# Flips, value products, narrowing and maxima's products one tile later, and scores tied behind groups, in a fused attention and two-MoE kernel

## The chip, the cores and the metric

One core of one Trainium2 chip runs the whole program. The metric is the device time of one execution in microseconds (us). Its engines are PE (TensorE, with PEld for its weight loads), DVE (VectorE), ACT (ScalarE), POOL (GpSimd) and SP (SyncE, which here issues DMAs). Each runs its own list of instructions in order and waits for the others by semaphores.

## The reference

The input is q, k, v of shape (4, 8, 576, 64) in float32 and the weights of two MoE layers in float64. What is computed:

```
q, k   = rotary(q), rotary(k)                      # cos/sin of position, per head
a      = softmax(q k^T / 8) v                      # 4 batches, 8 heads, 576 x 576
x      = a as 2304 tokens x 512
h      = max(x w1, x w2, x w3)                     # 512 -> 768, three products
y      = h w_out                                   # 768 -> 512        (first MoE)
t      = y w_in                                    # 512 -> 2048
out    = (t * sigmoid(t)) w_out                    # 2048 -> 512       (second MoE)
```

## The kernel before

**Tiles.** The attention works in 80 tiles, 20 for each batch (tiles 0 to 19 are batch 0, 20 to 39 batch 1, and so on). A tile is a batch, a pair of heads and a piece t of 128 query positions (t = 4 is half a piece: one instruction covers both heads). Batches come one after the other, each in two parts r: pieces 0 and 1 of all four head pairs, then pieces 2, 3 and 4.

**One tile.** `attention()` is a generator that gives out one tile's work at a step. `tile_scores` (lines L389 to L405) writes the scores of a tile into a PSUM tile `s`; there is only one, so the next score waits until the exponentials have read it. `tile_max` takes the row maxima on DVE (L414) and the exponentials on ACT (L421). One step later `tile_norm` takes the reciprocal (L431) and scales on ACT (L433), and `tile_move` sends the scaled exponentials by four DMAs on SP's queue into a transposed arrangement `pt` (for batches 1 to 3, which `moved(b)` says). Two steps later `tile_flip` transposes 32 x 32 blocks of `pt` on DVE (L494), and `tile_last` does the rest with PE (L483, L439). Batch 0 is transposed on PE alone (`tile_turn`, L504 to L521). When the pieces of a part are done, `av` multiplies by v (L535, L539) at the step that `av_at` gives, and writes the first MoE's input `x`.

**What is put between the tiles.** Behind each step the main loop gives out groups of the first MoE, a group being the products (L626) into one PSUM bank; a budget RATE of 8000 columns a tile sets how many, and `x_ready` from which step on a batch's part may be used. `up` evacuates its groups on ACT (L642) and DVE (L644), `down` on ACT (L668). The loop also steps through the narrowing of the second MoE's float64 weights to float32 (`narrow_w2`): load, a first step `narrow_a` on ACT (L214) and POOL (L216), a second step `narrow_b` on DVE (L225, L226), then the measuring of maxima and a store. After it `prep_w8` casts them in halves (L895 on ACT, L899 on DVE). The splits of the first MoE's output weights W_out1 into a high half (POOL, L160) and a low half (DVE, L163) are given out by `prep_wo1`. q and k are rotated on POOL (`rope_steps`, L330 ff.) and transposed (`qk_turn`, L351 to L374).

**Maxima.** `all_max` finds one maximum over 128 partitions: PE transposes the column of row maxima (L117), DVE reduces it (L119), and PE multiplies the result by a column of ones (L120) to spread it again; `scale_of` (L130 to L133) makes a scale of it.

**Order.** A scheduler decides the order of instructions on each engine from the order in which the code gives them out and a model of the engines. `tc.issue_after(x)` adds that an instruction stands behind x on its engine; `last[...]` holds the latest instruction of a kind. Pools of buffers (`Ring`) set how far ahead a step can be.

Of the kernel before, what the change touches and what calls it, by code (L numbers as in the profile page):

```python
# [17 lines left out]
P = 128  # L18
# [4 lines left out]
def fused_kernel(  # L23
# [65 lines left out]
    z64_p = right("z64_p", 3)  # L89
# [9 lines left out]
    cos_sb = once.tile([P, 9, D], F32, name="cos_sb")  # L99
    sin_sb = once.tile([P, 9, D], F32, name="sin_sb")  # L100
# [13 lines left out]
    def all_max(m):  # L114

        ps = (ps_am[0] if ps_am else ps_m).tile([P, 512], F32, tag="m", name="m")
# [4 lines left out]
        return ps[:, 256:257]  # L121

# [45 lines left out]
    class Weights:  # L168
# [68 lines left out]
        def scale(self, nm, lo=0, n=None, ma=None):  # L237
# [3 lines left out]
            self.s, self.inv = scale_of(all_max(m1), 1, nm, const)  # L241
            return self.s, self.inv

# [59 lines left out]
    def v_scale(b):  # L303
        ma = vmax_t.pop(b)
        m = small.tile([P, 1], F32, tag="vm1", name="vm1")
        nc.vector.tensor_reduce(out=m, in_=ma, op=ALU.max, axis=AX.X)
        sv_t[b] = scale_of(all_max(m), 1, "v")

    def qk_rope(b, hp):
        t = raw_t[b, hp]  # L310
        w = w_p.tile([P, 18, D], F32, tag="w", name="w")
        if b:
            with tc.issue_after(last["pool"]):
                return rope_steps(t, w, nc.gpsimd, ((0, 6), (6, 12), (12, 18)))
# [6 lines left out]
        return rope_steps(t, w, nc.gpsimd, ((0, 6), (6, 12), (12, 18)))  # L321

    def rope_steps(t, w, eng, parts):

        tt = eng.tensor_tensor
        for lo, hi in parts:
            r, v = t[:, lo:hi, :], w[:, lo:hi, :]
            t4, w4 = (x.rearrange("p (a h) d -> p a h d", h=2) for x in (r, v))
            sin2, cos2 = (x[:, lo // 2:hi // 2, :].unsqueeze(2).to_broadcast([P, (hi - lo) // 2, 2, D]) for x in (sin_sb, cos_sb))
# [247 lines left out]
    for b in range(1, B):  # L577
        u = first[b, 0]
        for hp in range(NP):
            at(u - 10 + hp if hp < 2 else u - 4, load_v, b, hp)  # L580
            at(u - 6 + hp + hp // 2 * 2, v_max, b, hp)
        at(u, v_scale, b)

    def attention():

        back = lambda j, n: tiles[j - n] if n <= j < len(tiles) + n else None
        for j in range(len(tiles) + 4):
            if j < len(tiles):
                tile_scores(tiles[j])
                tile_max(tiles[j])  # L590
            key = back(j, 2)
# [26 lines left out]
    def group(passes, n, ps=None, more=False):  # L618
# [6 lines left out]
        for i, (l, r) in enumerate(passes):  # L625
            nc.tensor.matmul(ps[:, 0:n], l, r, start=(first and i == 0), stop=(not more and i == len(passes) - 1))  # L626
# [145 lines left out]
    def narrow_w2(W, src, nm):  # L772
# [5 lines left out]
        for n in range(M + 4):  # L778
            if n >= 4:
                W.measure(n - 4)  # L780
                if nm == "wi":
                    i, o = divmod(n - 4, 2)
# [3 lines left out]
                        in_=W.t[n - 4].rearrange("p (f n) -> p f n", n=P),  # L786
                    )
                else:
                    nc.sync.dma_start(out=zscr[nm][:, (n - 4) * 256:(n - 3) * 256], in_=W.t[n - 4])
# [23 lines left out]
        W.scale("s" + nm, n=M)  # L813
# [424 lines left out]
    copy_tables()  # L1238
# [11 lines left out]
    at(3, v_scale, 0)  # L1250
# [136 lines left out]
```

## Time and profile before

| | before |
|---|---|
| time, median of 3 runs | 998.67 us (997.64 to 1002.69) |
| the profiled execution | 997.75 us, span 996.0 us |
| PE busy | 912.6 us (92% of the span) |
| PEld busy | 671.5 us (67%) |
| DVE busy | 698.1 us (70%) |
| ACT busy | 604.4 us (61%) |
| POOL busy | 494.0 us (50%) |
| DMA moved | 146.29 MB, 147 GB/s on average |

The span is the time from the first to the last instruction in the trace; the execution is somewhat longer. An engine's busy time counts the instructions that compute, not its waits. The shares are averages over the attention with the first MoE in between (the last tile's score starts at 573.14 us) and the second MoE after it, which have different limits.

### The profile page before, as it was taken

Reading aid. Unit: us, or ns where it says so; the run is one execution under the profiler, and the core shown is the slowest. Engines: PE = TensorE matmul, PEld = TensorE weight load, DVE = VectorE, ACT = ScalarE, POOL = GpSimd, SP = SyncE. Lnnn points to the kernel's source line nnn. Section 1 sums busy time; section 2 is a strip of 40 time slices with the busy share of each in tenths; the row PEclk is TensorE's granted clock in tenths of the full one; section 3 lists DMA queues with packets and bytes.
Section 4 is the critical chain, followed back from the end, with each engine's and each line's share of the span. In section 5 each row is a group of like instructions: output and inputs, shape, how many; then the busy total and the mean of one; then the engine's idle time right before and its main releaser. Section 6 shows DMA issues by size and latency. Waiting matters only on the chain.

```text
span 996.0 us, 19123 instructions
## 1 busy us (share of the span) xinstructions
PE 912.6 (92%) x6802; PEld 671.5 (67%) x6802; DVE 698.1 (70%) x1231; ACT 604.4 (61%) x1381; POOL 494.0 (50%) x548
## 2 busy tenths in 40 slices
PE   4677998899998999988998899999998999999997
PEld 2344665566664555655655567788887888888886
DVE  5669778677677666878777646754777767756554
ACT  2878677667676766778877734463464554554442
POOL 5835495891276401623234105653678258265264
PEclk9688899999999999999999999999999999999999
DMA  6943034878896967998999855263454254334101
GB/s 149 274 145 106 13 97 113 181 145 161 194 194 160 188 121 143 210 220 185 242 212 221 186 133 192 64 222 124 154 164 133 84 166 119 110 112 133 60 1 43
DMA packets 185198, 146.29 MB, mean 147 GB/s; under 512 B 51216, under 2 KB 168720, under 8 KB 185104
## 3 DMA queue, kind: packets, MB, share of 16 engines
q1 hardware_dynamic: 183600, 144.36, 57.8%
q8 instruction: 54, 0.88, 0.4%
q10 hardware_dynamic: 1504, 0.72, 0.3%
q14 instruction: 40, 0.33, 0.1%
HBM read 90.51 MB, written 26.21 MB: 117 GB/s over the span
## 4 chain that ended last, share of the span: by engine, by line
PE 37%; DMA 7%; DVE 4%; ACT 2%; POOL 2%; issue 2%; SPq 1%; DVEq 0%; ACTq 0%; POOLq 0%
PE m L1050 8%; PE mb L1050 6%; PE c L1113 4%; PE a L1113 4%; PE b L1113 4%; PE mg L626 3%; PE m L626 3%; PE d L1113 2%; DMA w8scr<-z 2%; POOL gsum L997 1%; DMA w8s<-w8scr 1%; DMA pt<-e 1%; PE m L1018 1%; PE mb L1018 1%; PE m L1113 1%
## 5 line engine op out<-in xcount | busy, mean ns | idle before, releaser
L626 PE MATMUL m<-x,w 128*128 128x256 f16 (+1 forms) x1388 | 193.7, 289 | 11.1 <-ACT t L642 4.3
L626 PEld LDWEIGHTS <-w 128*128 128x128 f16 x1632 | 160.7, 99 | 62.9 <-issue 19.0
L1113 PEld LDWEIGHTS <-g 128*128 128x128 f16 x1485 | 145.9, 98 | 17.3
L1050 PEld LDWEIGHTS <-w8s 128*128 128x128 f16 x1344 | 131.2, 98 | 16.1 <-issue 0.9
L891 POOL TENSOR_TENSOR z<-z 128x128 f32<-128x128 f32 (+1 forms) x96 | 61.7, 660 | 134.5 <-DMA z<-zwi 56.8
L421 ACT ACTIVATE e<-s,nb 128x576 f32<-128x576 f32 x144 | 105.2, 736 | 36.7 <-DVE nb L414 35.8
L414 DVE TENSOR_REDUCE nb<-s 128x2 f32<-128x1152 f32 (+1 forms) x80 | 98.5, 1232 | 29.3 <-PE s L404 24.1
L433 ACT ACTIVATE e<-e,rec 128x576 f32<-128x576 f32 x144 | 104.2, 767 | 10.0 <-DVE rec L431 9.9
L216 POOL TENSOR_SCALAR z<-z 128x256 uint16<-128x256 uint16 x64 | 54.1, 845 | 105.9 <-ACT z L214 77.8
L404 PE MATMUL s<-T 64*128 64x512 f32 x256 | 81.1, 695 | 0.0
L494 DVE STREAM_TRANSPOSE pt<-pt 128x1024 f32<-128x1024 f32 (+1 forms) x60 | 67.8, 1130 | 16.2 <-DMA pt<-e 15.6
L539 PE MATMUL xp<-pt,vd 128*64 128x256 f32 (+1 forms) x512 | 76.5, 415 | 0.5 <-DVE pt L494 0.5
L1064 POOL TENSOR_TENSOR z<-t 128x256 f32<-128x256 f32 x32 | 27.1, 847 | 89.2 <-DVE t L1056 54.1
L1002 DVE SCALAR_TENSOR_TENSOR g<-gsum,sg,g 128x1024 f16<-128x1024 f32 x36 | 49.5, 1382 | 23.1 <-ACT g L1001 22.6
L330 POOL TENSOR_TENSOR w<-qk,sin_sb 128x384 f32<-128x384 f32 (+1 forms) x44 | 46.0, 1065 | 35.4 <-DMA qk<-in_q_dram 24.0
L1001 ACT ACTIVATE g<-gsum,sg 128x1024 f16<-128x1024 f32 x36 | 40.8, 1140 | 35.9 <-POOL gsum L997 35.9
L626 PE MATMUL m<-h,wo 128*128 128x256 f16 (+1 forms) x448 | 60.8, 286 | 0.1
L539 PEld LDWEIGHTS xp<-pt,vd 128*64 128x64 f32 x512 | 35.3, 138 | 36.5 <-issue 13.3
L626 PEld LDWEIGHTS <-wo 128*128 128x128 f16 x512 | 49.7, 98 | 15.0 <-issue 1.7
L644 DVE SCALAR_TENSOR_TENSOR t<-m,t 128x256 f32<-128x256 f32 (+1 forms) x82 | 36.7, 447 | 18.9 <-PE m L626 11.6
L1113 PE MATMUL b<-w,g 128*128 128x256 f16 x376 | 48.5, 273 | 0.0
L1113 PE MATMUL c<-w,g 128*128 128x256 f16 x376 | 48.2, 275 | 0.0
(248 smaller groups left out, 1957.5 us busy)
## 6 DMA issues: line engine op xcount, KB each, us to landing
w8s<-w8scr SPq DMA_DIRECT2D x64, 448.0 KB, 4.2
pt<-e SPq DMA_DIRECT2D x192, 128.0 KB, 3.9
z<-in_moe_w_in_dram SPq DMA_DIRECT2D x32, 256.0 KB, 3.5
z<-in_moe_w_out_dram SPq DMA_DIRECT2D x32, 256.0 KB, 3.5
w<-in_moe_w_dram SPq DMA_DIRECT2D x6, 768.0 KB, 6.2
wo<-in_moe_w_dram SPq DMA_DIRECT2D x6, 768.0 KB, 4.7
qk<-in_q_dram SPq DMA_DIRECT2D x32, 128.0 KB, 3.4
vd<-in_v_dram SPq DMA_DIRECT2D x16, 256.0 KB, 3.4
```

The lines of the kernel that those rows point to most:

```text
L216: nc.gpsimd.tensor_scalar(out=q[:, :, 2], in0=q[:, :, 1], scalar1=step, scalar2=off, op0=ALU.mult, op1=ALU.add)
L404: last["s"] = last["score"] = nc.tensor.matmul(s[:, o:o + 512], qs[r], kt[r], start=True, stop=True).ins
L414: x = nc.vector.tensor_reduce(out=nb[:, 0:m], in_=both(s, 0, 960, 576) if m > 1 else s[:, 0:576], op=ALU.max, axis=AX.X, negate=True)
L421: x = nc.scalar.activation(out=e[:, HK[g]], in_=s[:, SK[g]], func=AF.Exp, bias=nb[:, g:g + 1], accum_out=sm[:, g:g + 1])
L433: nc.scalar.activation(out=e[:, HK[g]], in_=e[:, HK[g]], func=AF.Copy, scale=r[:, g:g + 1])
L494: nc.vector.transpose(out=x, in_=x)
L539: nc.tensor.matmul(xp[r, 0:n], v4[:, g, c, :], turned(c, g), start=False, stop=(c == 3))
L626: nc.tensor.matmul(ps[:, 0:n], l, r, start=(first and i == 0), stop=(not more and i == len(passes) - 1))
L891: nc.gpsimd.tensor_tensor(out=z[:, o], in0=z[:, x], in1=z[:, y], op=op)
L1002: nc.vector.scalar_tensor_tensor(out=l, in0=x, scalar=sg_t[jb], in1=h, op0=ALU.mult, op1=ALU.subtract)
L1050: nc.tensor.matmul(o, l, r, start=(i == 0), stop=(i == len(passes) - 1))
L1113: x = nc.tensor.matmul(ps, l, r, start=first, stop=last_, skip_group_check=True)
```

## The change

Seven things are edited.

1. The flips of batches 1 to 3 come three steps after the scores instead of two (`back(j, 3)`), and the value products `av` and the first use of the MoE's input one step later for these batches. The loop has one step more.
2. A score of batches 1 to 3 stands behind the last group given out (`issue_after(last["group"])`).
3. In `narrow_w2` the first step comes two steps after the load instead of one, the second three instead of two, the measuring and store five instead of four; the float64 tiles get a fourth buffer.
4. `all_max` is cut in two. For v and for the second MoE's weights the product that spreads the maximum is given out one step later, behind the last score.
5. The tables of cosines and sines hold 5 pieces instead of 9, and the copies that filled the rest on POOL are gone.
6. A rotary step on POOL works on pieces of 8, 8 and 2 instead of three of 6.
7. For batches 2 and 3 two of the four loads of v come one step later.

```diff
-    z64_p = right("z64_p", 3)
+    z64_p = right("z64_p", 4)
...
-    cos_sb = once.tile([P, 9, D], F32, name="cos_sb")
-    sin_sb = once.tile([P, 9, D], F32, name="sin_sb")
+    cos_sb = once.tile([P, 5, D], F32, name="cos_sb")
+    sin_sb = once.tile([P, 5, D], F32, name="sin_sb")
...
+    def max_bank():
+        return (ps_am[0] if ps_am else ps_m).tile([P, 512], F32, tag="m", name="m")
+
+    def all_max_a(m, ps=None):
+
+        ps = ps or max_bank()
         nc.tensor.transpose(ps[0:1, 0:P], m, ident)
         t = small.tile([1, 1], F32, tag="amax", name="amax")
         nc.vector.tensor_reduce(out=t, in_=ps[0:1, 0:P], op=ALU.max, axis=AX.X)
+        return t
+
+    def all_max_b(t, ps=None):
+
+        ps = ps or max_bank()
         nc.tensor.matmul(ps[:, 256:257], ones, t, start=True, stop=True)
         return ps[:, 256:257]
...
-            queue.dma_start(out=t[:, 4:9, :], in_=r[:, 4:9, :])
-
-    def copy_tables():
-        for t in (sin_sb, cos_sb):
-            nc.gpsimd.tensor_copy(out=flat(t[:, 0:4, :]), in_=flat(t[:, 4:8, :]))
+            queue.dma_start(out=t, in_=r[:, 4:9, :])
...
-        sv_t[b] = scale_of(all_max(m), 1, "v")
+        vmax_t[b] = all_max_a(m)
+
+    def v_scale_b(b):
+        with tc.issue_after(last["score"]):
+            sv_t[b] = scale_of(all_max_b(vmax_t.pop(b)), 1, "v")
...
-                return rope_steps(t, w, nc.gpsimd, ((0, 6), (6, 12), (12, 18)))
+                return rope_steps(t, w, nc.gpsimd, ((0, 8), (8, 16), (16, 18)))
...
-        av_at.setdefault(len(tiles) + 2, []).append((b, hp, r))
-        x_ready[b, r] = len(tiles) + 4
+        av_at.setdefault(len(tiles) + 2 + moved(b), []).append((b, hp, r))
+        x_ready[b, r] = len(tiles) + 4 + moved(b)
...
-            at(u - 10 + hp if hp < 2 else u - 4, load_v, b, hp)
+            at(u - 10 + hp if hp < 2 else u - 4 + (b > 1), load_v, b, hp)
...
         at(u, v_scale, b)
+        at(u + 1, v_scale_b, b)
...
-        for j in range(len(tiles) + 4):
+        for j in range(len(tiles) + 5):
             if j < len(tiles):
-                tile_scores(tiles[j])
+                with tc.issue_after(last["group"]) if tiles[j][0] else nullcontext():
+                    tile_scores(tiles[j])
                 tile_max(tiles[j])
-            key = back(j, 2)
+            key = back(j, 3)
             if key and moved(key[0]):
                 tile_flip(key)
...
-        for n in range(M + 4):
-            if n >= 4:
-                W.measure(n - 4)
+        for n in range(M + 5):
+            if n >= 5:
+                W.measure(n - 5)
...
+            if 3 <= n <= M + 2:
+                with tc.issue_after(last["max"]):
+                    W.narrow_b(n - 3, part.pop(n - 3, None))
             if 2 <= n <= M + 1:
-                with tc.issue_after(last["max"]):
-                    W.narrow_b(n - 2, part.pop(n - 2, None))
-            if 1 <= n <= M:
                 if wide:
-                    W.t[n - 1] = z_p.tile([P, 256], F32, tag="z", name="z")
+                    W.t[n - 2] = z_p.tile([P, 256], F32, tag="z", name="z")
                 with tc.issue_after(exps[-1]):
-                    W.narrow_a(n - 1, part.get(n - 1), pool=True)
+                    W.narrow_a(n - 2, part.get(n - 2), pool=True)
...
-        W.scale("s" + nm, n=M)
+        t = W.scale_a(n=M)
+        yield
+        with tc.issue_after(last["score"]):
+            W.scale_b("s" + nm, t)
         yield
```

What the scheduler makes of it shows at three places. The first is PE's order at the turn from batch 0 to batch 1. Here `s_1659` is the score of tile 20 and `s_1758` that of tile 21, `tr` are transposes, `m_1601` is the maximum of W_out1 and `m_1700` that of v. Before:

```order
L401 MATMUL s_1659<-kd_0_122,T_1380 128x2x64
L404 MATMUL s_1659<-T_1380 128x512 x2
L351 MATMUL tr_1573<-ident_78,qk_855 128x128 x4
L351 MATMUL tr_1567<-ident_78,qk_855 128x128 x4
L117 MATMUL m_1601<-ident_78,wm_2_1599 1x128
L515 MATMUL tr_1673<-ident_78,e_1454 128x128 x3
L365 MATMUL tr_1579<-ident_78,qk_855 128x128
L120 MATMUL m_1601<-amax_1603,ones_79 128x1
L117 MATMUL m_1700<-ident_78,vm_1_1698 1x128
L401 MATMUL s_1758<-kd_0_122,T_1380 128x2x64
```

After, the score of tile 20 is `s_1658`; `m_1600` is the maximum of W_out1, `m_1636` and `m_1727` are two `down` groups of batch 0, `h` their input, `wo1f` and `wo` the split pieces of W_out1:

```order
L128 MATMUL m_1600<-amax_1602,ones_79 128x1
...
L650 MATMUL m_1636<-h_0_973,wo1f_140 128x256
...
L650 MATMUL m_1727<-h_5_1521,wo_0_141 128x256
L650 LDWEIGHTS wo_0_141
L650 MATMUL m_1636<-h_5_1521,wo_0_141 128x256
L423 MATMUL s_1658<-kd_0_122,T_1379 128x2x64
L426 MATMUL s_1658<-T_1379 128x512 x2
L650 LDWEIGHTS wo_0_141
L650 MATMUL m_1727<-h_5_1521,wo_0_141 128x256
```

The score of tile 20 stood ahead of the product of W_out1's maximum; now it stands behind it and behind 35 of the 36 products of two groups that read W_out1's pieces.

The second place is DVE's order near tile 58. `nb` are row maxima, `pt_4596` is the buffer of tiles 54 to 56 of batch 2 (a flip of 1024 columns, or of 512 for tile 56, the half piece), `z` are pieces in narrowing. Before:

```order
L414 TENSOR_REDUCE nb_4886<-s_4882 128x2
L494 STREAM_TRANSPOSE pt_4596<-pt_4596 128x512
L150 TENSOR_REDUCE vmax_4538<-vd_0_128 128x1
L225 TENSOR_SCALAR z_4835<-z_4835 128x256
L899 SCALAR_TENSOR_TENSOR z_1_4634<-z_1_4634,wihalf_4125 128x512
```

After, `nb_4806` is the row maximum of tile 58, `nb_4886` that of tile 59, and `pt_4536` the buffer of tiles 54 to 56:

```order
L436 TENSOR_REDUCE nb_4806<-s_4802 128x2
L516 STREAM_TRANSPOSE pt_4536<-pt_4536 128x1024
L163 TENSOR_REDUCE vmax_4458<-vd_0_128 128x1
L238 TENSOR_SCALAR z_4743<-z_4743 128x256
...
L436 TENSOR_REDUCE nb_4886<-s_4883 128x1
L516 STREAM_TRANSPOSE pt_4536<-pt_4536 128x512
```

Behind the maximum of tile 58 stood the flip of tile 56; now it is the flip of tile 55, and that of tile 56 stands behind the next maximum.

The third place is PE's order at the last maximum, that of the second MoE's W_out (`wm_0`). `m_6677` before and `mg_6880`, `mg_6915` after are groups of the first MoE, `s_6627` is the score of tile 79. Before, the lines left out are the rest of one group:

```order
L117 MATMUL m_6665<-ident_78,wm_0_6663 1x128
L626 LDWEIGHTS w1f_137
L626 MATMUL m_6677<-x_5505,w1f_137 128x256
...
L120 MATMUL m_6665<-amax_6667,ones_79 128x1
L394 MATMUL s_6627<-T_5330,qd_0_121 128x512
```

After, the lines left out are the rest of `mg_6880` and further groups up to `mg_6915`:

```order
L650 MATMUL mg_6880<-x_5504,w_0_138 128x256
L120 MATMUL m_6700<-ident_78,wm_0_6698 1x128
...
L650 MATMUL mg_6915<-x_5504,w_0_138 128x256
L561 MATMUL xp_6747<-pt_6554,vd_0_129 64x320
L128 MATMUL m_6720<-amax_6702,ones_79 128x1
```

The transpose and the product of this maximum now lie further apart, and both come after the last score.

## Rows read from the trace of the kernel before

**Rows 1.** Windows: stretch, length, busy time of each engine, PE clock, DMA share, GB/s.

```profile
core 0: us, PE busy (x) PEld busy (x) DVE busy (x) ACT busy (x) POOL busy (x), PEclk, DMA share, GB/s
152.60:572.80 420.20, 385.31 (x2537) 243.34 (x2537) 310.47 (x575) 300.18 (x832) 178.72 (x221) 0.99 0.84 182
301.90:332.50 30.60, 24.26 (x138) 13.55 (x139) 20.15 (x43) 20.03 (x59) 15.08 (x19) 0.94 0.83 178
411.20:471.70 60.50, 49.99 (x342) 33.15 (x342) 49.63 (x96) 44.70 (x124) 24.44 (x37) 0.97 0.90 206
```

**Rows 2.** PE's waits, 152.6 to 573 us: us in total, times, longest.

```profile
PE s L401 <- ACT e L421: 8.8, 7, 1.6
PE s L394 <- ACT e L421: 6.8, 5, 3.8
PE m L626 <- DVE t L644: 4.4, 4, 1.6
PE m L120 <- DVE amax L119: 3.3, 1, 3.3
...
PE m L626 <- ACT t L642: 1.8, 2, 1.2
```

**Rows 3.** DVE's waits in the same stretch.

```profile
DVE pt L494 <- DMA pt<-e: 13.8, 11, 3.0
DVE z L226 <- POOL z L216: 11.6, 8, 4.4
```

**Rows 4.** Timeline of DVE: start, duration, instruction [idle before <- releaser].

```profile
524.95 1.25 DVE L494 STREAM_TRANSPOSE pt<-pt 128x1024 f32<-128x1024 f32 x1 [1.53 <-DMA pt<-e]
...
529.90 1.35 DVE L414 TENSOR_REDUCE nb<-s 128x2 f32<-128x1152 f32 x1
```

**Rows 5.** Timeline of ACT.

```profile
434.23 0.72 ACT L895 ACTIVATE w8o<-z,wihalf 128x512 f16<-128x512 f32 x1 [2.75 <-DMA w8scr<-w8o]
...
527.63 0.44 ACT L214 ACTIVATE z<-z 128x256 f32<-128x256 f32 x1 [2.30 <-DMA z<-in_moe_w_out_dram]
```

**Rows 6.** Timeline of PE at eight places.

```profile
158.47 0.39 PE L401 MATMUL s<-kd,T 128*128 128x128 f32 x2
...
307.73 0.49 PE L401 MATMUL s<-kd,T 128*128 128x128 f32 x2 [1.59 <-ACT e L421]
...
322.45 0.38 PE L401 MATMUL s<-kd,T 128*128 128x128 f32 x1 [1.45 <-ACT e L421]
...
436.55 1.84 PE L394 MATMUL s<-T,qd 128*128 128x512 f32 x2 [3.81 <-ACT e L421]
...
501.51 1.13 PE L404 MATMUL s<-T 64*128 64x512 f32 x4
...
502.73 1.79 PE L626 MATMUL m<-x,w 128*128 128x320 f16 x12
...
533.18 1.12 PE L394 MATMUL s<-T,qd 128*128 128x512 f32 x2 [2.07 <-ACT e L421]
...
572.83 0.38 PE L120 MATMUL m<-amax,ones 1*128 1x1 f32 x2 [3.27 <-DVE amax L119]
573.14 1.05 PE L394 MATMUL s<-T,qd 128*128 128x512 f32 x1
```

**Rows 7.** Timeline of POOL at the splits of W_out1.

```profile
165.34 0.69 POOL L160 TENSOR_SCALAR wo1f<-wo,swo1s 128x512 f16<-128x512 f32 x1 [6.26 <-DVE swo1i L133]
167.47 0.69 POOL L160 TENSOR_SCALAR wo<-wo,swo1s 128x512 f16<-128x512 f32 x1 [1.44 <-DVE wo L163]
```

**Rows 8.** Timeline of DVE at the first low half.

```profile
166.64 0.73 DVE L163 SCALAR_TENSOR_TENSOR wo<-wo,swo1s,wo1f 128x512 f16<-128x512 f32 x1
```

**Rows 9.** Window from score 19 on, columns as in rows 1.

```profile
152.90:174.00 21.10, 18.09 (x109) 10.54 (x107) 18.57 (x49) 15.30 (x40) 10.30 (x12) 1.00 0.49 118
```

**Rows 10.** POOL's groups by line and form: count, busy us, mean ns of one.

```profile
L330 POOL TENSOR_TENSOR w<-qk,sin_sb 128x384 f32<-128x384 f32 x42 | 44.6, 1081 | 31.8 <-DMA qk<-in_q_dram 24.0 <-DMA qk<-in_k_dram 5.5 <-issue 1.9
...
L1085 POOL TENSOR_TENSOR yr<-yr 128x512 f32<-128x512 f32 x8 | 12.3, 1553 | 0.1
```

**Rows 11.** Timeline of DVE: W_out2's scale, and its first use.

```profile
573.81 0.15 DVE L886 TENSOR_SCALAR wohalf<-swos 128x1 f32<-128x1 f32 x1
...
604.10 1.21 DVE L899 SCALAR_TENSOR_TENSOR w<-z,wohalf,w 128x768 f16<-128x768 f32 x1 [4.20 <-ACT w L895]
```

More of the change, by code (lines that the diff above doesn't have):

```diff
@@ L112, in fused_kernel @@
     ps_am = []
-    def all_max(m):
-        ps = (ps_am[0] if ps_am else ps_m).tile([P, 512], F32, tag="m", name="m")
+    def max_bank():
+        return (ps_am[0] if ps_am else ps_m).tile([P, 512], F32, tag="m", name="m")
+    def all_max_a(m, ps=None):
+        ps = ps or max_bank()
         nc.tensor.transpose(ps[0:1, 0:P], m, ident)
@@ L119, in all_max @@
         nc.vector.tensor_reduce(out=t, in_=ps[0:1, 0:P], op=ALU.max, axis=AX.X)
+        return t
+    def all_max_b(t, ps=None):
+        ps = ps or max_bank()
         nc.tensor.matmul(ps[:, 256:257], ones, t, start=True, stop=True)
         return ps[:, 256:257]
+    def all_max(m):
+        ps = max_bank()
+        return all_max_b(all_max_a(m, ps), ps)
     def scale_of(m, n, nm, pool=None):
@@ L235, in maxima, with row_max @@
             return ma
-        def scale(self, nm, lo=0, n=None, ma=None):
+        def row_max(self, lo=0, n=None, ma=None):
             ma = ma or self.maxima(lo, n or self.m)
@@ L240, in scale, with scale_a, scale_b @@
             nc.vector.tensor_reduce(out=m1, in_=ma, op=ALU.max, axis=AX.X)
-            self.s, self.inv = scale_of(all_max(m1), 1, nm, const)
+            return m1
+        def scale(self, nm, lo=0, n=None, ma=None):
+            self.s, self.inv = scale_of(all_max(self.row_max(lo, n, ma)), 1, nm, const)
             return self.s, self.inv
+        def scale_a(self, n):
+            return all_max_a(self.row_max(0, n))
+        def scale_b(self, nm, t):
+            self.s, self.inv = scale_of(all_max_b(t), 1, nm, const)
         def split(self, i, s=None, later=False):
@@ L320, in qk_rope @@
             return rope_steps(t, w, nc.vector, ((8, 16), (0, 8), (16, 18)))
-        return rope_steps(t, w, nc.gpsimd, ((0, 6), (6, 12), (12, 18)))
+        return rope_steps(t, w, nc.gpsimd, ((0, 8), (8, 16), (16, 18)))
     def rope_steps(t, w, eng, parts):
-        tt = eng.tensor_tensor
+        tt, at_ = eng.tensor_tensor, lambda c: 4 if c == 16 else c // 2 % 4
         for lo, hi in parts:
@@ L328, in rope_steps @@
             t4, w4 = (x.rearrange("p (a h) d -> p a h d", h=2) for x in (r, v))
-            sin2, cos2 = (x[:, lo // 2:hi // 2, :].unsqueeze(2).to_broadcast([P, (hi - lo) // 2, 2, D]) for x in (sin_sb, cos_sb))
+            sin2, cos2 = (x[:, at_(lo):at_(lo) + (hi - lo) // 2, :].unsqueeze(2).to_broadcast([P, (hi - lo) // 2, 2, D]) for x in (sin_sb, cos_sb))
             tt(out=w4, in0=t4, in1=sin2, op=ALU.mult)
@@ L625, in group @@
         for i, (l, r) in enumerate(passes):
-            nc.tensor.matmul(ps[:, 0:n], l, r, start=(first and i == 0), stop=(not more and i == len(passes) - 1))
+            x = nc.tensor.matmul(ps[:, 0:n], l, r, start=(first and i == 0), stop=(not more and i == len(passes) - 1))
+        last["group"] = x.ins
         return ps
@@ L785, in narrow_w2 @@
                         out=zscr[nm].rearrange("p (f c n) -> p f c n", c=KC, n=P)[:, 4 * q + 2 * o:4 * q + 2 * o + 2, c],
-                        in_=W.t[n - 4].rearrange("p (f n) -> p f n", n=P),
+                        in_=W.t[n - 5].rearrange("p (f n) -> p f n", n=P),
                     )
                 else:
-                    nc.sync.dma_start(out=zscr[nm][:, (n - 4) * 256:(n - 3) * 256], in_=W.t[n - 4])
+                    nc.sync.dma_start(out=zscr[nm][:, (n - 5) * 256:(n - 4) * 256], in_=W.t[n - 5])
+            if 3 <= n <= M + 2:
+                with tc.issue_after(last["max"]):
+                    W.narrow_b(n - 3, part.pop(n - 3, None))
             if 2 <= n <= M + 1:
-                with tc.issue_after(last["max"]):
-                    W.narrow_b(n - 2, part.pop(n - 2, None))
-            if 1 <= n <= M:
                 if wide:
-                    W.t[n - 1] = z_p.tile([P, 256], F32, tag="z", name="z")
+                    W.t[n - 2] = z_p.tile([P, 256], F32, tag="z", name="z")
                 with tc.issue_after(exps[-1]):
-                    W.narrow_a(n - 1, part.get(n - 1), pool=True)
+                    W.narrow_a(n - 2, part.get(n - 2), pool=True)
             if n < M:
@@ L1249, in fused_kernel @@
         at(hp * 2 // 3, v_max, 0, hp)
-    at(3, v_scale, 0)
+    at(2, v_scale, 0)
+    at(3, v_scale_b, 0)
     def moe_groups():
```

3 lines of the change are left out of this document (1 added, 2 removed).

## The prediction

> **What bounds the kernel now.** TensorE (PE) is the busiest engine by far, so I asked where it idles. After the attention the second MoE runs in an order that the change leaves alone, and through score 10 PE's order is the same too. So I cut out score 19 (152.6 us) to score 79 (572.8 us) in a table of windows [rows 1]. There PE is busy 385.31 of 420.20 us: 34.9 us is all that idle time can give back. Two stretches hold nearly half of it: 301.9 to 332.5 (24.26 busy of 30.60) and 411.2 to 471.7 (49.99 of 60.50), 16.9 us together.
>
> Next, what ended PE's waits in that stretch [rows 2]. Scores wait for the exponentials of the tile before (ACT, L421), which empty the one PSUM tile of scores: 8.8 + 6.8 = 15.6 us. Groups wait for their bank to be emptied: 4.4 + 1.8 = 6.2 us. One maximum's second product waits 3.3 us for DVE (VectorE). Why are the exponentials late? They need DVE's row maximum, and DVE executes its queue in order: it stands 13.8 us before transposes whose DMA has not landed, and 11.6 us in the narrowing [rows 3]. One tile shows the chain: DVE waits 1.53 us for the DMA of a flip at 524.95, and the row maximum of its queue starts at 529.90 [rows 4]; ACT waits 2.30 us for a load of W_out2 at 527.63 [rows 5]; PE then waits 2.07 us before the score at 533.18 [rows 6].
>
> **The change part by part.** *Flips and narrowing one tile later, value products with them.* No instruction is added; between a tile's DMA and its flip, and between a load and its first cast, lies one more tile (420.2 / 60 = 7.0 us). Eleven flips wait, at most 3.0 us [rows 3], so a tile more covers each. The value products move by the same tile, so they don't wait longer. What comes back is PE's time before scores. Of its 15.6 us I keep three waits: 1.59 and 1.45 us in the turn to batch 2, where PE has little queued, and 3.81 us before the score at 436.55 [rows 6], whose ACT had stood 2.75 us before a cast of the second MoE's weights, waiting for the store that frees its buffer [rows 5]. That is 6.85, and leaves 8.75: **-8.8**. Bounds: 0 (the loop score, maximum, exponential is the limit itself) and -15.6. The groups' 6.2 us wait for the same late engines; of DVE's 13.8 + 11.6 us of causes the flips are half, and the narrowing's wait for POOL (GpSimd) sits inside a step that moves as a whole and stays. So half: **-3.1**, bounds 0 and -6.2.
>
> *Scores behind groups.* PE's order becomes more even. A score is some 0.39 + 1.13 us, a group of twelve 320-column products 1.79 us [rows 6]; with every instruction at the duration of its like in the trace, of the 59 intervals from score 20 to score 78, 18 hold under 5 us of PE work before and 10 after, and 8 hold over 8 us before and 3 after. In a short interval PE runs dry before the exponentials are done: a second reason for the -8.8, no term of its own.
>
> *Maxima's products.* Before, the second product stood behind one group, with a score behind it, and waited 3.27 us at 572.83 [rows 6]. After, about two groups lie between: **-3.3**, bounds 0 and -3.3.
>
> The score behind that product started only after it, at 573.14 [rows 6]. The Trainium skill says so too (TensorE: Matmul & The Clock Gate, Part 2, "Step-by-step: what each phase is for"): matmuls stay in program order. By it a tied score inherits its group's waits, which speaks against the tie; by the rows alone I count 6 such waits, and what they would cost if all were passed on is a rival below.
>
> *The turn to batch 1.* Here the tie bites. Score 20 ran at 158.47 [rows 6]; after, it stands behind two groups of W_out1, 35 of their 36 products, which read all six of its split pieces. A piece's high half is written over the piece before it, so the splits run as one chain: POOL 0.69 us, DVE 0.73 us, POOL again (the second began at 167.47, 0.10 us after DVE's low half of the first ended) [rows 7, 8]. That is 0.69 + 0.73 + 2 x 0.10 = 1.62 us a piece, 9.7 us for six. The first began at 165.34; in the new order the row maximum of score 20 (1.35 us [rows 4]) no longer stands ahead of its scale on DVE, so 164.0. The last ends at 173.7 and score 20 starts at about 174, 15.5 us later. PE does not lose all of that: some 12.5 us of its work now lies between scores 19 and 20, all of which it can do by then, while before it was busy 18.09 us from 152.9 to 174.0 [rows 9]. The difference is **+6**. Bounds: +1 (the splits overlap: 6 x 0.69 + 0.73 = 4.9 us from 164.0, score 20 at 169) and +15.5 (the tiles never catch up). The intervals from score 20 to score 78 then hold 7 us less PE work, since 38 group products went ahead.
>
> *Clock.* The granted clock was 0.94 and 0.97 in the two idle stretches [rows 1]: 0.06 x 30.6 + 0.03 x 60.5 = 3.7 us. After the 3.81 us wait a score's products took 1.84 us, after the 2.07 us wait 1.12 [rows 6]. Fewer waits return a part: **-1**, bounds 0 and -3.7.
>
> *Costed at nothing.* Rotary on POOL goes from three pieces of 384 columns (1081 ns) to 512, 512 and 128. A 512-column operation of another line took 1553 ns [rows 10]; with under 0.5 us for the rest, 2 x 1.55 + 0.5 - 3 x 1.08 = 0.4 us per operation, 1.1 us per pair, 15 us for 14 pairs if nothing hid it. POOL is busy 24.44 of 60.50 us in its thinnest stretch [rows 1], and pairs are turned three tiles after, which hides it. The table copies go from POOL before any rotary step. Narrowing ends a few tiles later and with it W_out2's scale, ready at 573.81 and first used by a low half at 604.10 [rows 11]: 30 us cover it. Between scores 11 and 19 groups change places with transposes, but by score 19 the same 222 group products are issued. SP's DMAs are the same and in nearly the same places.
>
> Sum: -8.8 - 3.1 - 3.3 + 6 - 1 = -10.2. The profiled execution took 997.75 us (span 996.0), so 987.55; the median lies 0.9 above it: **988**.
>
> **Rivals.** *Nothing moves*, 998: the loop of a tile or DMA is the limit, and what the flips no longer wait for is waited for one step on. For: the DMA engines are busy 0.84 of the 420.20 us, 0.90 in the second stretch [rows 1], and later flips need no fewer bytes. Against: 0.84 x 420.2 is 353 us, so 67 us are free. All terms halved or cancelled by the turn: 994 to 1002.
>
> *Slower*, 1011: the lag of score 20 is never made up. Place: the first score of batch 1; price +15.5, less 3.3 for the maxima. It decides from a pace of 7 us a tile, that of before: with less PE work per interval (some 6.1 us) the tiles must run faster, or the lag stays whole. Against it: PE is the busiest engine, and its work was only brought forward.
>
> *Slower by passed-on waits*, 1008: each wait of a group, 6.2 us, now holds up the tied score behind it and with it the next maximum and exponentials, so that a score's wait follows each; then -8.8 and -3.1 turn into +6.2: 997.75 + 6.2 - 3.3 + 6 + 0.9, no clock gain. Against it: the groups' waits are 6 in 59 intervals [rows 2].
>
> *More*, 974: all of 15.6 + 6.2 + 3.3 = 25.1 us comes back, the turn costs +1 and the clock gives 1. Against it: the cast's wait and the thin turn are still there.
>
> **How the numbers follow.** Likeliest 0.43 (980 to 994), nothing 0.23, more 0.16, lag 0.11, passed-on 0.07. The range 972 to 1004 leaves out the lag, most of passed-on and a little below: under 2 in 10. A measurement of this kernel tells 0.5% (5 us) from no change. Faster, under 993.7: 0.41 + 0.16 + 0.02 = 0.59. Same: 0.02 + 0.21 + 0.01 = 0.24. Slower, over 1003.7: 0.17.
>
> **What the profile would show.** Right: PE's waits before scores between scores 19 and 79 under 8 us (from 15.6); DVE's waits for flips' DMAs near 0 (from 13.8); no 3 us wait at a maximum's product; score 20 near 174, score 79 near 563; from score 79 to the end the same 423 us within 2. Wrong: score 20 after 177 with tiles at 7 us (the lag), DVE's waits for flips gone while scores still wait 15 us (the loop), or groups' waits of more than 10 us with scores late behind them (passed on).

## The result: 0.7% slower where 1% faster was forecast

The changed kernel takes 1005.41 us (median of 9 runs, 1002.46 to 1009.69), the kernel before 998.67 in the same comparison: a ratio of 1.0068, 95% interval 1.0047 to 1.0089. The forecast was 988, its range ended at 1004.

The profiled execution of the changed kernel has a span of 1006.0 us, 10.0 over that of before; the medians differ by 6.7, so some 3 us of what follows belong to the two executions that were profiled. The starts of scores 19 and 79 in the two traces cut the difference into three stretches:

| | before | after | difference |
|---|---|---|---|
| start to score 19 | 152.9 | 148.9 | -4.0 |
| score 19 to score 79 | 420.2 | 428.2 | +8.0 |
| score 79 to the end | 422.9 | 428.9 | +6.0 |

The windows of the changed kernel show the turn to batch 1 (score 19 to 20), what follows it, the whole middle stretch and the end, with the columns of rows 1; the last line is the end of the kernel before:

```profile
148.95:173.35 24.40, 18.12 (x100) 10.82 (x99) 17.44 (x42) 9.44 (x26) 11.62 (x14) 0.84 0.36 93
173.35:210.00 36.65, 35.56 (x224) 22.42 (x225) 19.14 (x36) 24.07 (x64) 28.01 (x30) 0.92 0.56 117
...
148.90:577.10 428.20, 388.09 (x2549) 248.22 (x2547) 301.20 (x563) 299.31 (x826) 175.57 (x220) 0.97 0.79 176
...
577.10:1006.00 428.90, 414.48 (x3626) 356.43 (x3626) 279.96 (x474) 203.17 (x321) 223.93 (x234) 0.99 0.39 119
...
573.10:996.00 422.90, 412.27 (x3636) 356.20 (x3636) 274.83 (x460) 200.90 (x315) 220.37 (x233) 0.99 0.38 118
```

TensorE idles 428.2 - 388.1 = 40.1 us in the middle stretch, 34.9 before [rows 1], and its clock there is 0.97 on average, 0.99 before. In the turn it idles 6.3 us, at a clock of 0.84 on average.

TensorE's waits in the middle stretch of the changed kernel answer to rows 2:

```profile
PE s L423 <- ACT e L443: 7.2, 6, 2.1
PE m L650 <- DVE amax L122: 6.7, 2, 3.5
PE m L650 <- ACT t L667: 4.8, 3, 3.3
PE xp L561 <- DVE pt L516: 3.7, 3, 2.2
PE m L650 <- DVE ve L143: 3.5, 2, 2.0
PE m L650 <- DVE t L669: 3.5, 2, 2.3
PE tr L373 <- issue: 1.9, 1, 1.9
PE m L650 <- DVE wo L176: 1.7, 3, 1.2
PE m L650 <- POOL wo L173: 1.3, 3, 0.5
PE s L416 <- ACT e L443: 1.8, 3, 1.2
```

The kernel before has no group that waits for a reduction, and under half a microsecond of groups that wait for a scale, W_in's and v's:

```profile
PE m L626 <- DVE swie L130: 0.4, 1, 0.4
PE m L626 <- DVE ve L130: 0.3, 1, 0.3
```

VectorE's waits there, against rows 3:

```profile
DVE nb L436 <- PE s L426: 33.6, 25, 2.9
DVE x L565 <- ACT x L564: 23.2, 14, 3.7
DVE z L239 <- POOL z L229: 10.2, 6, 3.5
```

The first of these rows was, in the kernel before:

```profile
DVE nb L414 <- PE s L404: 15.4, 18, 2.0
```

What was forecast to go nearly went: scores wait 7.2 + 1.8 = 9.0 us instead of 15.6, VectorE's wait for the flips' DMA is not in the list at all (13.8 before), and no product of a maximum waits. But groups now wait for the maxima themselves: 6.7 us for the reduction (`amax`) and 3.5 us for the scale (`ve`), 10.2 us where before has 0.3. The groups' waits for evacuation grew too, 4.8 + 3.5 = 8.3 us against 6.2 [rows 2]. One maximum holds a group's bank from its transpose to the reduction, and a second one from its product to the scale; groups have two such banks. At batch 3 such a chain can be read. TensorE's timeline:

```profile
440.30 0.27 PE L120 MATMUL m<-ident,vm 128*1 128x128 f32 x1
443.88 1.47 PE L650 MATMUL m<-x,w 128*128 128x256 f16 x12 [3.32 <-ACT t L667]
448.51 2.38 PE L650 MATMUL m<-x,w 128*128 128x256 f16 x12 [3.15 <-DVE amax L122]
450.68 0.64 PE L423 MATMUL s<-kd,T 128*128 128x128 f32 x2
...
453.18 0.38 PE L128 MATMUL m<-amax,ones 1*128 1x1 f32 x2
453.49 1.48 PE L650 MATMUL m<-x,w 128*128 128x256 f16 x12
457.00 1.47 PE L650 MATMUL m<-x,w 128*128 128x256 f16 x12 [2.03 <-DVE ve L143]
```

VectorE's timeline of the same place:

```profile
442.12 0.43 DVE L676 TENSOR_TENSOR h<-t,h 128x256 f16<-128x256 f32 x1 [3.80 <-ACT h L675]
...
444.93 1.36 DVE L436 TENSOR_REDUCE nb<-s 128x2 f32<-128x1152 f32 x1
446.20 1.23 DVE L516 STREAM_TRANSPOSE pt<-pt 128x1024 f32<-128x1024 f32 x1
...
448.19 0.27 DVE L122 TENSOR_REDUCE amax<-m 1x1 f32<-1x128 f32 x1
```

The maximum's transpose was ready at 440.6, but its reduction stands behind a row maximum and a flip, in a queue that had waited 3.80 us for ScalarE before 442.12, and runs at 448.19; the second group after the transpose waits 3.15 us for it, and the score at 450.68, tied behind that group, comes 12 us after the one ahead of it (438.64).

In the last stretch TensorE idles 428.9 - 414.5 = 14.4 us, 10.6 before. Two waits stand out in its timeline; VectorE's follows:

```profile
588.50 1.12 PE L557 MATMUL xp<-pt,vd 128*128 128x320 f32 x2 [3.24 <-DVE pt L466]
...
618.25 2.13 PE L650 MATMUL m<-h,wo 128*128 128x256 f16 x15 [2.10 <-ACT h L675]
```

```profile
586.88 1.25 DVE L516 STREAM_TRANSPOSE pt<-pt 128x1024 f32<-128x1024 f32 x1 [2.21 <-DMA pt<-e]
```

The last value product waits 3.24 us; ahead of what it needs, VectorE waited 2.21 us for a flip's DMA, and no later tile is there to work on meanwhile.

### The profile page after: what moved, and what is told of

Its sections match the earlier page's. It is cut to its first block, busy times and chain, and to the rows that moved or that the text cites. A ratio compares the mean times of both kernels' runs of the same rounds, so it can differ in the third digit from the quotient of the medians.

```text
span 1006.0 us, 19143 instructions
## 1 busy us (share of the span) xinstructions
PE 912.4 (91%) x6802; PEld 674.0 (67%) x6802; DVE 693.5 (69%) x1231; ACT 605.3 (60%) x1381; POOL 493.6 (49%) x546
## 5 line engine op out<-in xcount | busy, mean ns | idle before, releaser
L650 PE MATMUL m<-h,wo 128*128 128x256 f16 (+1 forms) x448 | 63.9, 292 | 5.0 <-ACT h L675 2.1
L352 POOL TENSOR_TENSOR w<-qk,sin_sb 128x512 f32<-128x512 f32 (+2 forms) x44 | 44.3, 1023 | 47.4 <-DMA qk<-in_q_dram 28.6
L1141 PE MATMUL a<-w,g 128*128 128x256 f16 x376 | 48.4, 274 | 0.0
```

Source lines behind the costliest of these rows:

```text
L650: x = nc.tensor.matmul(ps[:, 0:n], l, r, start=(first and i == 0), stop=(not more and i == len(passes) - 1))
L1141: x = nc.tensor.matmul(ps, l, r, start=first, stop=last_, skip_group_check=True)
```

## The experiments

Ratios are to the kernel before, measured in turns on the same chip, with 95% intervals. Each comparison had 6 to 12 runs of a kernel. The intervals are some 2 us to either side, so a difference between two of these ratios is uncertain by some 3 us. The scheduler orders the whole program anew after each edit, so a single edit changes some order elsewhere too.

### Scores tied from tile 24 on

```diff
-                with tc.issue_after(last["group"]) if tiles[j][0] else nullcontext():
+                with tc.issue_after(last["group"]) if j >= 24 else nullcontext():
```

> The changed kernel with scores tied behind groups only from tile 24 on, so that scores 20 to 23 stand where they stood before; from about score 30 on the order of TensorE is that of the changed kernel. Theory 1 (the turn to batch 1 is the main cost: score 20 waits for the chain of splits, TensorE idles 6.3 us between scores 19 and 20 and its clock falls to 0.84 and 0.92 around it): score 20 at 155, score 24 ahead of 190 instead of 201, and some 11 us less than the changed kernel, 994 us. Theory 2 (the lag is made up by score 60 anyway, and the loss comes after it, from the maxima's banks and the tail): score 60 where it is now (438.7 us) and a time within 3 us of 1005.

0.9999 (0.9979 to 1.0019): the tie of the four scores 20 to 23 costs 0.69%, 6.9 us, where I had expected 11. Score 20 is at 155; score 24 at 194 is not ahead of 190. The turn's cost is gone here, so this kernel shows what the forecast gains came to: nothing. Its middle stretch in a window, and TensorE's waits there:

```profile
148.30:566.60 418.30, 385.11 (x2548) 246.36 (x2546) 306.71 (x563) 298.24 (x826) 175.41 (x220) 0.98 0.80 180
```

```profile
PE m L650 <- DVE amax L122: 5.4, 2, 3.5
PE m L650 <- ACT t L667: 4.7, 4, 3.6
PE s L423 <- ACT e L443: 4.3, 7, 1.4
PE m L650 <- DVE t L669: 4.1, 3, 2.3
PE m L650 <- DVE ve L143: 2.9, 2, 1.8
...
PE s L416 <- ACT e L443: 1.8, 3, 1.2
```

Scores wait 6.1 us, 9.5 less than before, but TensorE idles 33.2 us, only 1.7 less: groups wait 8.8 us for evacuation and 8.3 us for maxima.

### No tie

```diff
-                with tc.issue_after(last["group"]) if tiles[j][0] else nullcontext():
+                with nullcontext():
```

> The changed kernel with no score tied to a group; all else stays later. Theory 1 (the tie costs at the turn and gains elsewhere, since it was the even order that won back 22 us between scores 20 and 60): score 20 near 155, but a slower pace after it, and a time 3 us or more over that of the kernel tied from tile 24. Rival (the later flips and narrowing won it, the tie only costs): as fast as the kernel tied from tile 24, 994 us, or faster.

1.0055 (1.0035 to 1.0075): 5.6 us slower than with the tie from tile 24. On this base the tie gains.

### Maxima whole, with and without the turn

Transpose, reduction and product are given out together again, in one bank; the second kernel has the tie from tile 24 too.

```diff
-        vmax_t[b] = all_max_a(m)
-
-    def v_scale_b(b):
-        with tc.issue_after(last["score"]):
-            sv_t[b] = scale_of(all_max_b(vmax_t.pop(b)), 1, "v")
+        sv_t[b] = scale_of(all_max(m), 1, "v")
...
-        t = W.scale_a(n=M)
-        yield
-        with tc.issue_after(last["score"]):
-            W.scale_b("s" + nm, t)
+        W.scale("s" + nm, n=M)
...
```

> The changed kernel with the maxima whole again (transpose, reduction and product in one PSUM bank, given out together, as before). Theory 1 (the split maximum takes two of the two banks that the groups use, and groups wait 10.2 us for its reduction and its scale): these waits go, one wait of about 3 us at a product comes back, and score 62 follows score 60 in 14 us instead of 22: about 7 us less, 998 us. Rival (whoever waits, the maximum is late because VectorE's queue is): the waits come back at the products, and the time stays within 3 us of 1005.

> The changed kernel tied from tile 24 and with whole maxima: both suspected costs away, flips, value products and narrowing still later. If both costs are real and add up: 1005 - 11 - 7 = 987 us, faster than before. If they are made up elsewhere: 998 or more, and then the tail behind score 79 (428.9 us, 422.9 before) is what is left.

1.0053 (1.0031 to 1.0076) and 0.9998 (0.9977 to 1.0020). The groups' waits for maxima are gone, and this row of TensorE's waits stands in the first kernel instead:

```profile
PE m L128 <- DVE amax L122: 7.0, 2, 4.1
```

Beside a tie, whole maxima give back 1.5 us or nothing: whether a group or the product waits, the reduction is late in VectorE's queue. The rival held; the two costs did not add up to 18 us.

### Flips, narrowing and tie alone on the kernel before

The first has the diff's lines on `back`, `av_at`, `x_ready` and the loop's length, and leaves the loads of v where they were, so that some value products read values of the next batch. The second has the short tables, the rotary pieces and `narrow_w2` with whole maxima. The third:

```diff
-                tile_scores(tiles[j])
+                with tc.issue_after(last["group"]) if j >= 24 else nullcontext():
+                    tile_scores(tiles[j])
...
```

> The kernel before with only the flips, value products and the first use of the MoE's input one tile later for batches 1 to 3. Theory 1 (the flips' DMA waits, 13.8 us of VectorE's time, held up maxima, exponentials and scores): 5 us or more faster than before. Theory 2 (those waits were slack, another operand of the same tile comes last in their place, and at the end of the attention the later flips find no work to cover them): no gain up to score 79, and some 4 us lost after it, 1000 us beside 996.

> The kernel before with the short tables, the rotary pieces of 8, 8 and 2, the narrowing one tile later and its fourth buffer; maxima whole, flips and scores as before. Theory 1 (the 4 us by which the changed kernels reach score 10 earlier come from the table copies that are gone, and narrowing is hidden): score 10 at 84 instead of 88 and 4 us faster at the end, 992. Theory 2 (the start is taken back later or was chance of that profile): within 2 us of before.

> The kernel before with only the scores from tile 24 on tied behind the last group given out. Theory 1 (the even order is what gains: without the tie the changed kernel lost 5 us against the one tied from tile 24): 5 us faster than before, 991. Theory 2 (the tie only makes up for what the later flips and value products cost, by putting groups where TensorE would idle): within 2 us of before.

Flips 1.0042 (1.0019 to 1.0065), narrowing and tables 0.9965 (0.9941 to 0.9990), tie 1.0100 (1.0067 to 1.0132). The flips' kernel decides against my first step. Its middle stretch in a window, TensorE's waits, then VectorE's:

```profile
152.10:578.80 426.70, 396.71 (x2513) 247.03 (x2511) 306.38 (x571) 298.92 (x831) 176.74 (x221) 0.97 0.82 179
```

```profile
PE s L401 <- ACT e L421: 16.0, 6, 4.1
...
PE s L394 <- ACT e L421: 2.3, 4, 0.8
```

```profile
DVE nb L414 <- PE s L404: 27.3, 28, 4.2
DVE z L226 <- POOL z L216: 19.3, 9, 3.6
DVE kd L374 <- ACT qd L369: 14.5, 7, 4.2
```

No wait for the flips' DMA is left among them, but scores still wait 18.3 us (15.6 before). VectorE waits for GpSimd's narrowing 19.3 us instead of 11.6 [rows 3]. Idle time did come back, though: TensorE idles 30.0 us in this stretch, 34.9 before. The stretch is 6.5 us longer all the same, since TensorE is busy 11.4 us longer in it, with no more instructions (2513, 2537 before) and at a clock of 0.97 instead of 0.99. The loss lies before score 79, not behind it as my second theory had it. The tie alone costs more than the whole change, so it is no gain by itself.

### The last batch's flips at their former steps

```diff
-        av_at.setdefault(len(tiles) + 2 + moved(b), []).append((b, hp, r))
-        x_ready[b, r] = len(tiles) + 4 + moved(b)
+        av_at.setdefault(len(tiles) + 2 + (0 < b < 3), []).append((b, hp, r))
+        x_ready[b, r] = len(tiles) + 4 + (0 < b < 3)
...
-            key = back(j, 3)
-            if key and moved(key[0]):
-                tile_flip(key)
+            for n in (3, 2):
+                key = back(j, n)
+                if key and moved(key[0]) and (key[0] < 3) == (n == 3):
+                    tile_flip(key)
```

> The changed kernel tied from tile 24, with the flips, value products and use of the input of the last batch at their steps of before (batches 1 and 2 stay one tile later). Theory 1 (the later flips cost at the end of the attention, where no tile follows that covers them: 428 us from score 79 to the end against 423): the tail falls to 424 and the time to 992. Theory 2 (the tail is longer since W_out2's maximum and the last groups come later): the tail stays at 428 and the time at 996.

0.9997 (0.9978 to 1.0017), while the profile has 423.7 us from score 79 to the end instead of 428.0. The tail is shorter, the time not measurably so.

### Tables alone, split maxima alone, flips without the later groups

`b_tables` has the lines on tables and rotary pieces, `b_split` those on maxima, `flips_x4` the flips' lines without `x_ready` and with the loads of v.

> The kernel before with only the short tables (no copies on GpSimd) and the rotary pieces of 8, 8 and 2; narrowing as before. Theory 1 (the 0.35% that tables and narrowing won together is the start: the copies that are gone): score 10 at 84 us instead of 88 and the time 3 to 4 us under before. Rival (narrowing one tile later won it): score 10 at 84, but within 2 us of before at the end.

> The kernel before with only the maxima in two parts, in a bank each, the product one step later behind the last score. Theory 1 (two banks for a maximum cost more than the wait at its product, here without the tie): about 5 us slower than before, with groups waiting for the reduction and the scale. Rival (my forecast: the product's wait of 3.3 us goes and nothing comes): 3 us faster. Second rival: within 2 us, since what waits changes and not how late the maximum is.

> The kernel before with flips and value products one tile later and the two loads of v with them, but the MoE's input used from the same step on as before. Theory 1 (the later flips alone cost 4 us since the groups of batches 1 to 3 start a tile later and fewer of them are issued by a given score, 1236 products instead of 1284 by score 60): the count by score 60 is 1284 again and the time within 2 us of before. Rival (the loop of a tile itself got longer, with scores still waiting 18 us for exponentials): as slow as with the later use, 1001.

Tables 1.0003 (0.9982 to 1.0024): score 10 comes 4.7 us earlier in the profile, and the lead is gone by the end; so it was mostly the narrowing that won the 0.35%, as far as two intervals tell that just overlap. Split maxima 1.0039 (1.0020 to 1.0058), where I had forecast a gain of 3.3 us. Flips 1.0086 (1.0065 to 1.0107): not the groups' later start makes them slow. In this kernel VectorE waits for the narrowing 11.4 us, much as before, and scores wait 13.0 us, less than before; yet it is the slower of the two with the flips alone. TensorE idles 28.2 us from score 19 to score 79 and is busy 396.8 us, at a clock of 0.97: again the idle time fell and the busy time rose.

### Without tie, maxima whole

> The changed kernel without the tie and with whole maxima, so flips, value products, narrowing and tables later or shorter. If the single edits add up (flips +4.2, tables and narrowing -3.7 us), it stands at 997, within 2 us of before. If the split maxima are not what makes the kernel without a tie slow, it stays at 1001.

0.9981 (0.9963 to 0.9998), about as the single edits add up. Against the kernel without tie (1.0055), split maxima cost 7.4 us here, though no wait for a reduction stands in that kernel's list. Its middle stretch is 8.5 us longer, and 6.9 us of them are busy time of TensorE (394.4 against 387.5), with as many instructions (2525 and 2524) and no lower a clock (0.98 against 0.97); why, I have not found. Two timelines of this kernel show what holds VectorE at one place, GpSimd's first, then VectorE's:

```profile
323.64 1.26 POOL L348 TENSOR_TENSOR w<-qk,sin_sb 128x512 f32<-128x512 f32 x1 [6.14 <-DMA qk<-in_q_dram]
324.99 1.83 POOL L229 TENSOR_SCALAR z<-z 128x256 uint16<-128x256 uint16 x2
```

```profile
325.78 0.42 DVE L239 SCALAR_TENSOR_TENSOR z<-z,z 128x256 int32<-128x256 int32 x1 [5.93 <-POOL z L229]
326.12 0.78 DVE L671 TENSOR_TENSOR h<-t,h 128x320 f16<-128x320 f32 x1
326.82 1.35 DVE L432 TENSOR_REDUCE nb<-s 128x2 f32<-128x1152 f32 x1
```

GpSimd waits 6.14 us for q, the narrowing stands behind the rotary step, VectorE waits 5.93 us for the narrowing, and the row maximum stands behind that.

### Rotary later, narrowing on ScalarE, last batch as before

All three on the kernel of the section above.

```diff
-            at(j - 3, qk_rope, b, hp)
+            at(j - 2, qk_rope, b, hp)
...
-        at(u - 6 if i > 3 else i - 4, qk_rope, b, hp)
+        at(u - 5 if i > 3 else i - 4, qk_rope, b, hp)
```

```diff
-                    W.narrow_a(n - 2, part.get(n - 2), pool=True)
+                    W.narrow_a(n - 2, part.get(n - 2))
```

> The changed kernel without the tie and with whole maxima (0.9981 of before), and the rotary steps of batches 1 to 3 one step later, one step nearer to their transposes. Theory 1 (what took the flips' place in VectorE's queue is the narrowing's wait for GpSimd, which stands at rotary steps whose q and k have not landed, 6.1 us at 323.64): VectorE's waits for z fall from 19.2 us to under 8, and the time by 4 us or more, 0.994 of before. Rival (the loop of a tile is the limit whoever holds VectorE): waits for z fall but the time stays within 2 us. Second rival: the pairs are then late for their transposes, and TensorE waits before them instead.

> The same base, with the second part of the narrowing's first step on ScalarE instead of GpSimd, so that VectorE never waits for GpSimd there. Theory 1: waits for z 19.2 us to near 0; ScalarE gets 64 steps of some 0.5 us more in 420 us of which it is busy 300; the time falls by 3 us or more. Rival (ScalarE, on which the exponentials stand, is the limit by then): slower by 5 us or more.

> The same base, with the flips, value products and use of the input of the last batch at their steps of before. Theory 1 (the later steps of the last batch cost at the end): from score 79 to the end 422 us instead of 426.7, and the time 0.9935 of before. Rival (the tail varies with the number of groups left over): within 2 us of the base.

Rotary later: 0.9994 (0.9978 to 1.0010), VectorE's wait for GpSimd 17.5 us instead of 19.2; it missed its target. Narrowing on ScalarE: 0.9965 (0.9947 to 0.9983); the wait is gone, scores wait 8.1 us for exponentials instead of 12.6, and 4.8 us elsewhere; the gain over the base lies within the intervals. Last batch as before: 0.9950 (0.9932 to 0.9969), though the tail fell only from 426.7 to 425.0 and the middle stretch from 416.6 to 411.6, not where I had expected it. TensorE runs 36 instructions fewer in the middle stretch (2488 against 2524) and as many more behind it; at 1.47 us for twelve products that is 4.4 us of work by my estimate, so the place says little.

### Splits earlier, and the faster version

The first is the changed kernel with

```diff
-        next(wprep2, None)
+        for _ in range(2):
+            next(wprep2, None)
```

> The changed kernel, tie and split maxima and all, with W_out1's loading, narrowing and splits given out two steps a tile instead of one, so that the splits are done about a tile earlier. Score 20 stays tied behind the same 35 products. Theory 1 (at the turn the tie costs because those products wait for the chain of splits): score 20 near 158 instead of 173 and a time within 2 us of the kernel tied from tile 24 (0.9999 of before). Rival (the tie costs at the turn whatever it waits for, since groups stand ahead of the first scores of the batch and the attention starves later): the time stays over 1.004 of before.

1.0070 (1.0045 to 1.0095). Score 20 comes at 168.68 and nothing waits for more than 0.7 us on the splits:

```profile
164.91 0.28 PE L650 MATMUL m<-h,wo 128*128 128x256 f16 x1 [0.68 <-DVE wo L176]
...
168.68 0.39 PE L423 MATMUL s<-kd,T 128*128 128x128 f32 x2
```

Score 20 was expected near 158. The middle stretch is 7.5 us shorter in its profile, but score 19 is 4.1 us later, and by the median nothing is gained. So the chain of splits is not shown to be what the tie of scores 20 to 23 costs; whether those 4.1 us are the price of the earlier loads, or of the groups ahead, stays open.

The other two are the last batch's version of the section above (0.9950) with the narrowing on ScalarE, and with whole maxima, last batch as before and the tie from tile 24.

> The version without tie, with whole maxima and the last batch's flips at their former steps (0.995 of before), and the narrowing's second part on ScalarE (0.9965 against 0.9981 on its base). If the two gains add: 0.9934. If the wait for GpSimd only passes to the next late operand: 0.995.

> The same version with the tie from tile 24 (0.9998 of before with the last batch later). If the tie gains nothing once the maxima are whole: 0.997 or more, worse than without the tie (0.995). If it evens out TensorE's order as I forecast: under 0.993.

0.9890 (0.9865 to 0.9914) and 1.0051 (1.0028 to 1.0074). The first, at 985.73 us (996.26 for the kernel before there), is faster than both kernels, and than either of its expectations (0.9934 and 0.995): on this base the narrowing on ScalarE gains 0.6%, clear of the intervals, where it gained 0.16% on the other. So VectorE's wait for GpSimd does cost in this version. Its middle stretch, in windows:

```profile
150.70:563.40 412.70, 388.06 (x2538) 244.94 (x2536) 307.91 (x575) 333.27 (x898) 123.96 (x157) 0.99 0.84 185
```

TensorE idles 24.6 us there, against 34.9 and 40.1, at a clock of 0.99. The tie costs 1.0% on the base of both (0.9950 to 1.0051).

## Why the prediction was wrong, step by step

The result is, within the intervals, the turn's cost and nothing else. Without the tie of scores 20 to 23 the kernel stands at 0.9999; with it 6.9 us are added, and 5.5 (0.9998 to 1.0053) where the maxima are whole. So the turn cost what was forecast, and all the gains, -16.2 us in the sum, came to -0.1.

Measured kernels make a chain from before to after, each one edit on: narrowing and tables -3.5 us, flips and value products +1.6, split maxima +7.4, the tie from tile 24 on -5.6, the tie of scores 20 to 23 +6.9. They sum to +6.8, the measured change. What a middle step is worth hangs on the order: with the tie from tile 24 on put ahead of the split maxima, it costs 1.7 us and they cost 0.1. By these runs:

- **Flips: -8.8 for scores and -3.1 for groups. Nothing came back.** Measured +1.6 on the narrowing's base, within the intervals, +4.2 and +8.6 us alone. The step that failed is "What comes back is PE's time before scores": it counted a wait that goes as time that is won. The flips' waits did go, in the changed kernel and alone, and tied scores wait 9.0 us instead of 15.6, or 6.1 with the tie from tile 24 on. But TensorE's idle time over the stretch is 40.1 and 33.2 us, against 34.9: it idles before groups instead. With the flips alone scores still wait 18.3 or 13.0 us; 4.9 and 6.7 us of idle time come back there, and 11.4 and 11.5 us more busy time take more than that. The clock, 0.97 for 0.99, is worth up to some 8.5 us of it in those profiles (0.02 x 426.7, an estimate from rounded clocks); why it fell is open. Behind the flip's DMA stands the narrowing's wait for GpSimd in VectorE's queue, which I had in view (11.6 us [rows 3]); it grew to 19.3 us in one of the two kernels and not in the other, slower one (11.4), so it is not shown to be what the flips cost.
- **Maxima's products: -3.3. Wrong sign.** The wait at the product went as forecast. The step that failed is that "about two groups lie between" was all I looked at: a maximum in two parts takes two banks from the two that groups have, and groups wait for its reduction and scale, 10.2 us in the changed kernel. With the tie, undoing it moves the wait back to the product and gains 1.5 us at most; alone on the kernel before it costs 3.9 us and without the tie 7.4, with no such wait in the latter, and how is open.
- **The turn: +6. Right in size, in part by luck.** Score 20 came at 173.3 (forecast 174), TensorE idled 6.3 us ahead of it, and the tie of scores 20 to 23 costs 6.9 us. But score 19 came 4.0 us earlier than before, so score 20 stood 24.4 us behind it and not 21.1, and TensorE was busy 18.1 us between them, at a clock of 0.84, where I had counted some 12.5 us. The chain of splits is not shown to be the reason: with the splits early the wait goes, but the time stays.
- **Scores behind groups: no term of its own. Wrong.** It swings most, and by the rest of the kernel: from tile 24 on -5.6 us where maxima are split, +1.7, within the intervals, where they are whole, +10.0 alone on the kernel before, +10.1 on the version with whole maxima and the last batch as before. Groups ahead of a score can fill TensorE where it would wait, and can delay a score that was ready; what decides between the two, these runs do not tell. VectorE's row maxima wait 33.6 us for scores in the changed kernel, but 32.1 us in the one without the tie, so the tie is not what makes that row.
- **Clock: -1. Wrong sign.** 0.97 against 0.99 over the middle stretch: (1 - clock) times length, summed over five windows of each, is 10.8 us against 5.0, and most of the difference lies at the turn (0.84 and 0.92).
- **Tables at nothing, narrowing inside the -8.8.** Together they gained 3.5 us, mostly the narrowing. The tail, forecast unchanged within 2 us, grew by 6.0, and score 79 came at 577.1 where 563 was forecast.

Of the rivals, "nothing moves" is what the kernel tied from tile 24 on shows; with the turn's cost on top it is the result. The lag was not kept: score 20 was 14.9 us late, score 60 is 7.3 us earlier than before. The sign named for passed-on waits did appear: groups wait over 20 us, and a tied score follows late. But 10.2 us of that wait came from the maxima, which that rival did not have, and the time, 1005, was reached by another sum than its 1008. The score at 450.68 shows the mechanism: it started only after the group ahead of it, which waited 3.15 us. That matmuls stay in program order is also what the Trainium skill states (TensorE: Matmul & The Clock Gate, Part 2, "Step-by-step: what each phase is for"). The bounds of single terms were too tight: they ended at the wait removed on the side of gains, and at nothing on the side of losses, and the maxima's term came out as a loss, as did the flips' on the kernel before.

## What to carry to other kernels

A row of waits that goes is not time that is won: here scores' waits went and TensorE idled before groups instead, or was busy longer. List what each engine would wait for next, and check a change by the busiest engine's idle time, busy time and clock over a whole stretch, not by one row. Before a step is cut in two, count the buffers that each half holds and who else takes them; a wait that leaves one row may return in another row that the trace of before doesn't have. Test edits in combination too: a tie that gains 0.6% on one version cost 1.0% on another, and the fastest version here took the plain parts (narrowing later and off GpSimd, flips later except in the last batch) and left tie and split maxima out; whether it needs the later flips was not tested.

## What was unexpected

The granted clock was 0.84 on average in a stretch where TensorE was busy for 18.1 of 24.4 us, and 0.92 over the next 36.7 us, in which it was busy for 35.6. Executions of one kernel on one core lay up to 1.1% apart (991.3 to 1002.3 us for the tie from tile 24 with whole maxima), so that a single profile, 989.5 us there, says little about a difference of 5 us.
